# Batch 0's v cast by the DMA, its q and k on the other queue, and the first two gate and value tiles begun on half of their channels

## The chip, the cores and the metric

The kernel runs on one core of one Trainium2 chip. The metric is the device time of one execution in microseconds (us). A kernel is run several times beside runs of the kernel before on the same chip. "Span" is the part of an execution that the profile covers, some 1.8 us less than its time.

The core's engines are TensorE (PE, with its weight loads as PEld), VectorE (DVE), ScalarE (ACT), GpSimd (POOL) and SyncE (SP). Two kinds of DMA queue matter. Loads issued from SyncE go to a hardware queue (q1 in the trace) and arrive as they are. Loads issued from GpSimd go to a software queue (q0), which can also cast fp32 to fp16 on the way.

## The reference

```python
# q, k, v: (8 batches, 8 heads, 576 rows, 64), fp32
kv  = einsum('bhsd,bhse->bhde', k, v)              # one 64x64 state per batch and head
o   = einsum('bhsd,bhde->bhse', q, kv)
x   = o / sqrt(mean(o*o over the head) + 1e-6) * g_norm
x   = x.transpose(0, 2, 1, 3).reshape(4608, 512)   # 512 channels = 8 heads x 64
h   = gelu(x @ w_gate) * (x @ w_val)               # 512 -> 1536, twice
out = x + sigmoid(x @ w_res) * (h @ w_out)         # 1536 -> 512
```

## The kernel before

One batch is one "block" of 512 tokens (rows 0 to 511 of its 576). The remaining 64 rows of all batches are gathered into a ninth block. While TensorE does the feed-forward work of block b, the attention of batch b+1 is slipped in between ("plan"). Only batch 0 has nothing before it to hide behind, so it is done in two halves of four heads each, and those first 26 us are what most of the change is about.

The loads of batch 0. All three tensors come as fp32 on SyncE's queue in halves; the remaining 64 rows of k and v come on GpSimd's queue, cast, as `kl` and `vl`:

```python
for half in range(2):
    lo, hi = half * HH, (half + 1) * HH
    for which, t in (("q", q), ("k", k), ("v", v)):
        nc.sync.dma_start(out=raw[0, which][:, lo:hi, :], in_=rows4(t, 0, lo, hi))
# ... g_norm, three small loads on SyncE
load_last_kv(0)          # kl, vl: k and v of rows 512 to 575, all eight heads, on GpSimd
```

k-times-v of a half needs five matmuls for each pair of heads: four over the 512 rows, then one over the remaining rows, in the same accumulation.

```python
for j in range(NJ):
    nc.tensor.matmul(ps, lhsT=k16[:, j, cs], rhs=v16[:, 2*pr : 2*pr+2, j*D : (j+1)*D],
                     start=(j == 0), stop=False)
nc.tensor.matmul(ps, lhsT=kl[:, cs], rhs=vl[:, cs], start=False, stop=True)
```

The order of the start, cut. `keep_warm(n)` issues n multiplications of zeros, which are to keep TensorE's clock up (a run below shows it, with a clock of 1.00 against 0.50):

```python
f_cast("q", 0, nc.scalar.copy)
f_cast("k", 0, nc.vector.tensor_copy)
f_qT(0)                                  # transposes of q
...
f_cast("v", 0, nc.gpsimd.tensor_copy)
keep_warm(3)
f_kv(0); f_kv_out(0)                     # k-times-v of half 0, masked
f_o(0, 0, 2, ...); f_o(0, 2, 2, ...)     # outputs of half 0
f_sq; f_red; f_sqrt; f_t                 # squares, sums, root, t = o / rms
f_cast("k", 1, nc.gpsimd.tensor_copy)
for i in range(len(WCS)):
    load_wgv(i)                          # weights of gate and value, on GpSimd
...
f_cast("v", 1, nc.vector.tensor_copy)
f_kv(1); f_kv_out(1)                     # half 1, its normalisation token block by token block
```

The first two gate and value tiles are then made for each token block j over all four channel chunks at once, after the block's transposes:

```python
for j in range(NJ):
    after(j)                             # transposes and evacuation of token block j
    for f in range(2):
        m_mm(tiles[2*f],     wg_c, f, blk, j, j + 1)    # 128x128, channels 0 to 511
        m_mm(tiles[2*f + 1], wv_c, f, blk, j, j + 1)
```

## Time and profile before

| | before |
|---|---|
| median, all runs beside the changed kernel | 375.12 us (374.72 to 375.77, 4 runs) |
| span of the profiled run, mean granted TensorE clock | 373.6 us, 0.993 |
| TensorE busy | 358.0 us, 96% |
| mask of half 0's k-times-v starts | 10.52 us |
| gate and value tile 2 starts (TensorE dense from here) | 26.55 us |
| block 1 starts | 64.78 us |

The last three rows are read from the time order of the instructions (start, length, instruction, and in brackets the idle time before it and what ended it); two of them are:

```profile
10.52 0.42 DVE L458 TENSOR_TENSOR kv<-kvp,mask 128x256 f16<-128x256 f32 x1 [3.42 <-PE kvp L168]
64.78 1.04 PE L286 MATMUL gps<-xT,wg 128*128 128x512 f16 x4
```

They cut the run into pieces that can be judged alone. Up to the mask it is loading that counts; from mask to tile 2 the chain of half 0, half 1 and normalisation; from tile 2 to block 1 the stalls around batch 1's attention. From the start of block 1 on, the kernel takes 308.8 us (373.6 - 64.78).

### The profile page before, as it was taken

How to read it: one execution, taken by the hardware profiler on the slowest of the kernel's cores; microseconds unless marked ns; L12 is line 12 of the kernel's file. 1: busy time of each engine (PE TensorE's matmuls, PEld its weight loads, DVE VectorE, ACT ScalarE, POOL GpSimd, SP SyncE). 2: the span in 40 equal slices, each digit the busy share in tenths (PEclk: the TensorE clock that was granted, in tenths of full speed). 3: DMA queues.
4: the chain of work that ended last, by engine and by line, in shares of the span. 5: the costliest groups of instructions: out<-in, count | busy, mean ns of one | idle time of the engine just before them, and what ended most of it. 6: DMA issues, size and time to landing. Idle time of an engine off the chain costs nothing.

```text
span 373.6 us, 5442 instructions
## 1 busy us (share of the span) xinstructions
PE 358.0 (96%) x2120; PEld 180.6 (48%) x2120; DVE 215.6 (58%) x427; ACT 153.2 (41%) x257; POOL 47.0 (13%) x65
## 2 busy tenths in 40 slices
PE   6779999999999999999999999999999999999993
PEld 2554464554455455545464445444644444444441
DVE  2566448778546946584657664756478453343422
ACT  3563373453346344544364335533563333123310
POOL 3843140500050002200130005000000000000000
PEclk9899999999999999999999999999999999999998
DMA  9999997590159012901192029601000200020013
GB/s 246 187 202 197 198 200 74 81 221 2 58 107 141 0 56 63 182 5 56 61 172 18 28 84 133 58 31 56 30 0 2 84 29 2 28 80 7 0 43 70
DMA packets 49452, 30.76 MB, mean 82 GB/s; under 512 B 14098, under 2 KB 44818, under 8 KB 49426
## 3 DMA queue, kind: packets, MB, share of 16 engines
q0 software_dynamic: 40848, 17.83, 38.2%
q1 hardware_dynamic: 8578, 12.59, 9.6%
q8 instruction: 16, 0.26, 0.3%
q14 instruction: 10, 0.08, 0.1%
HBM read 38.80 MB, written 9.44 MB: 129 GB/s over the span
## 4 chain that ended last, share of the span: by engine, by line
PE 90%; DVE 5%; DMA 2%; ACT 1%; issue 1%; SPq 0%; DVEq 0%
PE gps L286 25%; PE vps L286 24%; PE fps L331 24%; PE rps L318 8%; DMA qf<-in_q_dram 2%; PE xtp L260 2%; PE kvp L161 2%; PE qtp L151 2%; PE op L190 2%; DVE t L501 1%; DVE pf L337 1%; DVE ss L485 1%; ACT xT L521 1%; PE orp L208 0%; PE kvp L168 0%
## 5 line engine op out<-in xcount | busy, mean ns | idle before, releaser
L286 PE MATMUL gps<-xT,wg 128*128 128x512 f16 (+1 forms) x456 | 112.6, 368 | 2.0 <-ACT xT L521 1.5
L275 DVE TENSOR_TENSOR hid<-ge,vps 128x512 f16<-128x512 f16 x108 | 73.6, 685 | 68.0 <-PE vps L286 67.8
L286 PE MATMUL vps<-xT,wv 128*128 128x512 f16 (+1 forms) x456 | 111.9, 368 | 0.0
L274 ACT ACTIVATE ge<-gps 128x512 f16<-128x512 f32 x108 | 64.5, 598 | 99.7 <-PE gps L286 92.9
L331 PE MATMUL fps<-wo,hid 128*128 128x512 f16 x432 | 99.6, 379 | 0.0
L286 PEld LDWEIGHTS <-wv 128*128 128x128 f16 x456 | 43.6, 98 | 50.2 <-issue 0.2
L331 PEld LDWEIGHTS <-hid 128*128 128x128 f16 x432 | 42.0, 98 | 49.3
L286 PEld LDWEIGHTS <-wg 128*128 128x128 f16 x456 | 41.8, 98 | 42.7 <-issue 2.6
L337 DVE SCALAR_TENSOR_TENSOR pf<-th,fps 128x512 f32<-128x512 f32 x36 | 24.5, 688 | 59.4 <-PE fps L331 59.4
L318 PE MATMUL rps<-wr,xT 128*128 128x512 f16 x144 | 36.9, 379 | 0.1
L327 ACT ACTIVATE th<-rps 128x512 f32<-128x512 f32 x36 | 21.5, 598 | 37.7 <-PE rps L318 37.7
L261 ACT ACTIVATE xT<-xtp,gcol 128x512 f16<-128x512 f16 x32 | 20.5, 685 | 37.6 <-PE xtp L260 37.6
L99 POOL DMA_DIRECT2D qraw<-in_q_dram x7 | 6.3, 894 | 162.0 <-DVE q L106 126.8
L342 DVE SCALAR_TENSOR_TENSOR osb<-pf,t 128x512 f32<-128x512 f32 x36 | 24.9, 691 | 1.1
L184 DVE TENSOR_REDUCE ss<-sq 128x8 f32<-128x512 f32 x32 | 21.9, 686 | 5.5 <-ACT sq L183 3.0
L183 ACT ACTIVATE sq<-op 128x512 f32<-128x512 f32 x28 | 16.8, 598 | 12.0 <-PE op L190 12.0
L318 PEld LDWEIGHTS <-xT 128*128 128x128 f16 x144 | 13.2, 98 | 13.9 <-issue 1.5
L248 DVE TENSOR_TENSOR t<-op,ny 128x512 f16<-128x512 f32 x28 | 17.9, 683 | 0.3
L152 ACT COPY qT<-qtp 128x1024 f16<-128x1024 f16 x14 | 14.2, 1013 | 9.1 <-PE qtp L151 9.1
L161 PE MATMUL kvp<-v,k 128*128 128x128 f16 x128 | 10.9, 222 | 3.3 <-POOL v L434 2.2
L267 DVE TENSOR_TENSOR t<-t,g 128x512 f16<-128x512 f16 x36 | 13.5, 418 | 0.0
L190 PEld LDWEIGHTS <-qT 128*128 128x128 f16 x112 | 8.6, 98 | 6.6
(82 smaller groups left out, 203.4 us busy)
## 6 DMA issues: line engine op xcount, KB each, us to landing
out_dram<-osb SPq DMA_DIRECT2D x32, 256.0 KB, 2.3
qraw<-in_q_dram POOLq DMA_DIRECT2D x7, 512.0 KB, 6.0
kraw<-in_k_dram POOLq DMA_DIRECT2D x7, 512.0 KB, 7.9
v<-in_v_dram POOLq DMA_DIRECT2D x7, 512.0 KB, 9.8
wo<-in_moe_w_out_dram POOLq DMA_DIRECT2D x3, 512.0 KB, 13.8
qf<-in_q_dram SPq DMA_DIRECT2D x2, 512.0 KB, 7.6
kf<-in_k_dram SPq DMA_DIRECT2D x2, 512.0 KB, 6.5
vf<-in_v_dram SPq DMA_DIRECT2D x2, 512.0 KB, 7.8
```

The lines of the kernel that those rows point to most:

```text
L161: nc.tensor.matmul(ps, lhsT=k16[:, j, cs], rhs=v16[:, 2 * pr : 2 * pr + 2, j * D : (j + 1) * D], start=(j == 0), stop=False,)
L184: nc.vector.tensor_reduce(out=st[b]["ss"][:, j, :], in_=sq, op=ALU.add, axis=mybir.AxisListType.X)
L248: nc.vector.tensor_tensor(out=t_t[blk][:, jj, :].rearrange("p (h d) -> p h d", h=H), in0=s["o"][j].rearrange("p (h d) -> p h d", h=H), in1 ...
L261: nc.scalar.activation(out=xT_t[blk][:, :, jj * P : (jj + 1) * P], in_=ps, func=AF.Copy, scale=gcol)
L274: nc.scalar.activation(out=ge, in_=gps, func=AF.Gelu)
L275: nc.vector.tensor_tensor(out=hids[blk][:, f, :], in0=ge, in1=vps, op=ALU.mult)
L286: nc.tensor.matmul(ps[:, j0 * P : j1 * P], lhsT=w[:, cc, :], rhs=xT_t[blk][:, cc, j0 * P : j1 * P], start=(cc == 0), stop=(cc == NP - 1),)
L318: nc.tensor.matmul(rps, lhsT=xT_t[blk][:, cc, j * P : (j + 1) * P], rhs=wr16[:, cc, :], start=(cc == 0), stop=(cc == NP - 1),)
L327: nc.scalar.activation(out=th, in_=rps, func=AF.Tanh, scale=0.5)
L331: nc.tensor.matmul(fps, lhsT=hids[blk][:, f, j * P : (j + 1) * P], rhs=wo16[:, f, :], start=(f == 0), stop=(f == NF - 1))
L337: nc.vector.scalar_tensor_tensor(out=pf, in0=th, scalar=1.0, in1=fps, op0=ALU.add, op1=ALU.mult)
L342: nc.vector.scalar_tensor_tensor(out=osb, in0=pf, scalar=0.5, in1=t_t[blk][:, j, :], op0=ALU.mult, op1=ALU.add)
```

## The change

The intent has three parts. (1) *Loads*: v is cast by the DMA on GpSimd's queue, which takes two casts off GpSimd and VectorE; q and k stay on SyncE's queue. (2) *Start*: the accumulation of tiles 0 and 1 over channels 0 to 255 (half 0) is put under the normalisation of half 1, so that only channels 256 to 511 remain for the four serial rounds. (3) *Plan*: batch 1's attention becomes one clump after the residual matmuls of block 0.

```diff
-        for which, t in (("q", q), ("k", k), ("v", v)):
+        for which, t in (("q", q), ("k", k)):
             nc.sync.dma_start(...)
+    load_v0(0)                        # v, heads 0 to 3, on GpSimd, cast by the DMA
     ... g_norm, on SyncE
-    load_last_kv(0)
     make_identity(nc, ident32)
+    load_last_kv(0)
+    load_v0(HH)                       # v, heads 4 to 7
 ...
-    f_cast("v", 0, nc.gpsimd.tensor_copy)
-    keep_warm(3)
+    keep_warm(6)
     f_kv(0)
     f_kv_out(0)
 ...                                  (k's second half: cast by VectorE, q's by GpSimd)
-    f_cast("v", 1, nc.vector.tensor_copy)
+    keep_warm(5)
     f_kv(1)
 ...                                  (half 1 is normalised in two pairs, not four blocks)
+        for f in range(2):
+            m_mm(tiles[2 * f], wg_c, f, 0, 0, NJ, 0, 2)       # 128x512, channels 0 to 255
+            m_mm(tiles[2 * f + 1], wv_c, f, 0, 0, NJ, 0, 2)
+        for j in range(NJ):
+            f_xT(1, j, 1, pattn, "at")
+            f_xT_out(1, j, 1, j == NJ - 1)
+            for f in range(2):
+                m_mm(tiles[2 * f], wg_c, f, 0, j, j + 1, 2, NP)
+                m_mm(tiles[2 * f + 1], wv_c, f, 0, j, j + 1, 2, NP)
 ...
+    def attn_plan_1():                (both transposes of q, k-times-v and the remaining
+        ...                            rows in one slot; the multiplications by g in block 1)
```

More of the change, by code (lines that the diff above doesn't have):

```diff
@@ L281, in w_of, with m_mm @@
         return ws[i][:, :, o : o + P]
-    def m_mm(ps, ws, f, blk, j0, j1):
+    def m_mm(ps, ws, f, blk, j0, j1, c0=0, c1=NP):
         w = w_of(ws, f)
-        for cc in range(NP):
+        for cc in range(c0, c1):
             nc.tensor.matmul(
@@ L290, in m_mm @@
                 start=(cc == 0),
-                stop=(cc == NP - 1),
+                stop=(cc == NP - 1 and j1 == NJ),
             )
@@ L301, in m_gval @@
         m_act(blk, f, gps, vps)
-    def m_gval_first(blk, after):
-        hids[blk] = hidp.tile([P, NF, NJ * P], FP16, tag="hid", name="hid")
-        tiles = [pmoe.tile([P, NJ * P], FP32, tag="mm", name=n) for n in ("gps", "vps", "gps", "vps")]
-        for j in range(NJ):
-            after(j)
-            for f in range(2):
-                m_mm(tiles[2 * f], wg_c, f, blk, j, j + 1)
-                m_mm(tiles[2 * f + 1], wv_c, f, blk, j, j + 1)
-        for f in range(2):
-            m_act(blk, f, tiles[2 * f], tiles[2 * f + 1])
     def m_res(blk, j):
@@ L378, with load_v0 @@
     raw[0, "q"] = stage.tile([P, H, NJ * D], FP32, name="qf")
-    for which in "kv":
-        t = hidp.tile([P, NF, NJ * P], FP16, tag="hid", name=which + "f")
-        t = t.rearrange("p a b -> p (a b)").bitcast(FP32)[:, 0 : H * NJ * D]
-        raw[0, which] = t.rearrange("p (h x) -> p h x", h=H)
-    for half in range(2):
-        lo, hi = half * HH, (half + 1) * HH
-        for which, t in (("q", q), ("k", k), ("v", v)):
-            nc.sync.dma_start(out=raw[0, which][:, lo:hi, :], in_=rows4(t, 0, lo, hi))
+    t = hidp.tile([P, NF, NJ * P], FP16, tag="hid", name="kf")
+    t = t.rearrange("p a b -> p (a b)").bitcast(FP32)[:, 0 : H * NJ * D]
+    raw[0, "k"] = t.rearrange("p (h x) -> p h x", h=H)
+    for lo in (0, HH):
+        for which, t in (("q", q), ("k", k)):
+            nc.sync.dma_start(out=raw[0, which][:, lo : lo + HH, :], in_=rows4(t, 0, lo, lo + HH))
+    def load_v0(lo):
+        nc.gpsimd.dma_start(out=b16_t[0, "v"][:, lo : lo + HH, :], in_=rows4(v, 0, lo, lo + HH))
+    load_v0(0)
     gcol = consts.tile([P, 1], FP32, name="gcol")
@@ L428, with f_cast @@
     first = {}
-    def f_cast(which, half, copy):
-        hs = slice(half * HH, (half + 1) * HH)
-        dst, src = b16_t[0, which], raw[0, which]
-        if which == "v":
-            copy(out=dst[:, hs, :], in_=src[:, hs, :])
-        else:
-            copy(
-                out=dst.rearrange("p j h d -> p h j d")[:, hs, :, :],
-                in_=src.rearrange("p h (j d) -> p h j d", j=NJ)[:, hs, :, :],
-            )
+    def f_cast(which, lo, hi, copy):
+        hs = slice(lo, hi)
+        copy(
+            out=b16_t[0, which].rearrange("p j h d -> p h j d")[:, hs, :, :],
+            in_=raw[0, which].rearrange("p h (j d) -> p h j d", j=NJ)[:, hs, :, :],
+        )
     def f_qT(half):
@@ L494, in f_sqrt, with f_rinv @@
         nc.scalar.activation(out=rms0[at], in_=s0["ss"][at], func=AF.Sqrt, bias=eps_col, scale=1.0 / D)
+    def f_rinv(half, j0, n):
+        hs = slice(half * HH, (half + 1) * HH)
+        nc.vector.reciprocal(out=rinv0[:, j0 : j0 + n, hs], in_=rms0[:, j0 : j0 + n, hs])
     def f_t(half, j0, n):
@@ L498, in f_t @@
         ps = first["o", half, j0]
-        nc.vector.reciprocal(out=rinv0[:, j0 : j0 + n, hs], in_=rms0[:, j0 : j0 + n, hs])
         for j in range(n):
@@ L506, in f_t, with f_xT_tile, f_xT_pe @@
             )
-    def f_xT(half, j0, n, pool, tag):
-        first["xT", half, j0] = ps = pool.tile([P, 2, n, P], FP16, tag=tag, name="xtp")
+    def f_xT_tile(half, j0, n, pool, tag):
+        first["xT", half, j0] = pool.tile([P, 2, n, P], FP16, tag=tag, name="xtp")
+    def f_xT_pe(half, j0, n):
+        ps = first["xT", half, j0]
         for j in range(n):
@@ L513, in f_xT @@
                 nc.tensor.transpose(ps[:, e2, j, :], t0[:, j0 + j, cc * P : (cc + 1) * P], ident)
+    def f_xT(half, j0, n, pool, tag):
+        f_xT_tile(half, j0, n, pool, tag)
+        f_xT_pe(half, j0, n)
     def f_xT_out(half, j0, n, on_vector):
@@ L523 @@
     keep_warm(10)
-    f_cast("q", 0, nc.scalar.copy)
-    f_cast("k", 0, nc.vector.tensor_copy)
+    f_cast("q", 0, HH, nc.scalar.copy)
     f_qT(0)
+    f_cast("k", 0, HH, nc.vector.tensor_copy)
     f_qT_out(0, nc.scalar.copy)
     f_qT_out(1, nc.vector.tensor_copy)
-    f_cast("v", 0, nc.gpsimd.tensor_copy)
-    keep_warm(3)
+    keep_warm(6)
     f_kv(0)
     f_kv_out(0)
-    f_cast("q", 1, nc.scalar.copy)
+    keep_warm(2)
     f_o(0, 0, 2, pmoe, "mm")
     f_o(0, 2, 2, pmoe, "mm")
+    f_cast("q", HH, H, nc.gpsimd.tensor_copy)
+    for i in range(len(WCS)):
+        load_wgv(i)
     f_sq(0, 0, 2)
+    f_sq(0, 2, 2)
     f_red(0, 0, 2)
+    f_red(0, 2, 2)
+    f_sqrt(0, 0, 2)
+    f_sqrt(0, 2, 2)
+    keep_warm(4)
     f_qT(1)
     f_qT_out(2, nc.scalar.copy)
-    f_qT_out(3, nc.vector.tensor_copy)
-    f_cast("k", 1, nc.gpsimd.tensor_copy)
-    for i in range(len(WCS)):
-        load_wgv(i)
-    load_qr(0)
-    f_sqrt(0, 0, 2)
-    f_t(0, 0, 2)
-    f_sq(0, 2, 2)
-    f_red(0, 2, 2)
-    f_sqrt(0, 2, 2)
-    keep_warm(8)
-    f_cast("v", 1, nc.vector.tensor_copy)
+    f_qT_out(3, nc.scalar.copy)
+    f_cast("k", HH, H, nc.vector.tensor_copy)
+    f_rinv(0, 0, 2)
+    f_t(0, 0, 2)
+    keep_warm(5)
     f_kv(1)
@@ L555 @@
     f_xT_out(0, 0, 2, False)
+    f_rinv(0, 2, 2)
     f_t(0, 2, 2)
-    for j in range(NJ):
-        f_o(1, j, 1, pattn, "at")
-    f_sq(1, 0, 1)
-    f_sq(1, 1, 1)
-    f_red(1, 0, 1)
-    f_sqrt(1, 0, 1)
-    f_t(1, 0, 1)
-    keep_warm(2)
-    f_xT(0, 2, 2, pmoe, "mm")
-    f_sq(1, 2, 1)
-    f_xT(1, 0, 1, pattn, "at")
-    f_xT_out(1, 0, 1, False)
-    f_red(1, 1, 1)
-    f_sqrt(1, 1, 1)
-    f_t(1, 1, 1)
-    f_xT_out(0, 2, 2, False)
-    f_sq(1, 3, 1)
-    f_red(1, 2, 1)
-    def first_chunk(j):
-        if j == 1:
-            f_xT(1, 1, 1, pattn, "at")
-            f_xT_out(1, 1, 1, False)
-            f_sqrt(1, 2, 1)
-            f_t(1, 2, 1)
-            f_red(1, 3, 1)
-        elif j == 2:
-            f_xT(1, 2, 1, pattn, "at")
-            f_sqrt(1, 3, 1)
-            f_xT_out(1, 2, 1, False)
-            f_t(1, 3, 1)
-            nc.scalar.preload_act_table_set("gelu_and_others")
-        elif j == 3:
-            f_xT(1, 3, 1, pattn, "at")
-            f_xT_out(1, 3, 1, True)
-            nc.vector.memset(ones16, 1.0)
-            nc.vector.tensor_copy(out=grow16, in_=grow[:, None, :].to_broadcast([1, H, D]))
-            for t in last_kv[1]:
-                nc.vector.memset(t[R:P], 0.0)
-            for t in qtr:
-                nc.vector.memset(t, 0.0)
@@ new lines, with first_gval @@
+    f_o(1, 0, 2, pattn, "at")
+    f_o(1, 2, 2, pattn, "at")
+    f_sq(1, 0, 2)
+    f_sq(1, 2, 2)
+    f_xT(0, 2, 2, pattn, "at")
+    f_xT_out(0, 2, 2, False)
+    f_red(1, 0, 2)
+    f_sqrt(1, 0, 2)
+    f_red(1, 2, 2)
+    f_sqrt(1, 2, 2)
+    f_rinv(1, 0, 2)
+    f_t(1, 0, 2)
+    f_rinv(1, 2, 2)
+    f_t(1, 2, 2)
+    keep_warm(6)
+    def first_gval():
+        hids[0] = hidp.tile([P, NF, NJ * P], FP16, tag="hid", name="hid")
+        tiles = [pmoe.tile([P, NJ * P], FP32, tag="mm", name=n) for n in ("gps", "vps", "gps", "vps")]
+        for f in range(2):
[4 more added lines that the diff above has]
+            f_xT_out(1, j, 1, j == NJ - 1)
+            if j == NJ - 1:
+                nc.scalar.preload_act_table_set("gelu_and_others")
+            for f in range(2):
+                m_mm(tiles[2 * f], wg_c, f, 0, j, j + 1, 2, NP)
+                m_mm(tiles[2 * f + 1], wv_c, f, 0, j, j + 1, 2, NP)
+        for f in range(2):
+            m_act(0, f, tiles[2 * f], tiles[2 * f + 1])
+        load_qr(0)
+        nc.vector.memset(ones16, 1.0)
+        nc.vector.tensor_copy(out=grow16, in_=grow[:, None, :].to_broadcast([1, H, D]))
+        for t in last_kv[1]:
+            nc.vector.memset(t[R:P], 0.0)
+        for t in qtr:
+            nc.vector.memset(t, 0.0)
@@ L605, in g_rows, with attn_plan_1 @@
         nc.vector.tensor_copy(out=g16, in_=ps)
+    def attn_plan_1():
+        b = 1
+        o = [lambda j=j: a_o(b, j) for j in range(NJ)]
+        t = [lambda j=j: a_t(b, j) for j in range(NJ + 1)]
+        x = [lambda j=j: a_xT(b, j) for j in range(NJ + 1)]
+        plan = {
+            NF - 1: [lambda: by_token(b, "q")],
+            NF: [lambda: by_token(b, "k")],
+            NF + 3: [
+                lambda: attn_begin(b),
+                lambda: a_qT(b, 0),
+                lambda: a_qT(b, 1),
+                lambda: load_batch(b + 1),
+                lambda: a_kv(b, 0, NP),
+                lambda: a_rem_qT(b),
+            ],
+            NF + 4: [lambda: a_rem_o(b), o[0]],
+            NF + 5: [o[1]],
+            NF + 6: [o[2]],
+            NF + 7: [o[3]],
+            NF + 8: [lambda: a_norm(b), t[0], t[1], t[2], t[3], t[4]],
+            2 * NF + 1: [x[0], x[1]],
+            2 * NF + 2: [x[2], x[3]],
+            2 * NF + 3: [x[4]],
+        }
+        return plan, [lambda j=j: a_x(b, j) for j in range(NJ + 1)]
     def attn_plan(b):
@@ L636 @@
         if blk == 0:
-            slots = [lambda: m_gval_first(0, first_chunk), None]
+            slots = [first_gval, None]
             slots += [lambda f=f: m_gval(0, f) for f in range(2, NF)]
@@ L645 @@
             slots += [lambda j=j: m_out(blk, j) for j in range(NJ)]
-            for j, f in enumerate(late):
-                plan[j] = [f]
+            for j, fs in enumerate(late):
+                plan[j] = list(fs)
             late = []
-        if blk + 1 < B:
+        if blk == 0:
+            new_block(1)
+            more, rows = attn_plan_1()
+            for i, fs in more.items():
+                plan.setdefault(i, []).extend(fs)
+        elif blk + 1 < B:
             new_block(blk + 1)
             for i, fs in enumerate(attn_plan(blk + 1)):
-                plan.setdefault((NF - 1 if blk == 0 else 0) + i, []).extend(fs)
+                plan.setdefault(i, []).extend(fs)
         for s in range(len(slots)):
@@ L658 @@
             if blk == 0 and s == 2:
+                nc.gpsimd.dma_start(out=wr16, in_=moe_w_res.rearrange("(cc p) c -> p cc c", p=P))
                 load_batch(1)
-                nc.gpsimd.dma_start(out=wr16, in_=moe_w_res.rearrange("(cc p) c -> p cc c", p=P))
                 for f in range(0, NF, 4):
@@ L664 @@
         if blk == 0:
-            late = stores
+            late = [[g] for g in stores] + [[] for _ in range(NJ)]
+            for j, g in enumerate(rows):
+                late[j + 2].append(g)
 _INS = ['q', 'k', 'v', 'g_norm', 'moe_w_gate', 'moe_w_val', 'moe_w_out', 'moe_w_res']
```

## The prediction

> **What bounds the kernel now.** I first read the busy shares of the page.
>
> ```profile
> PE 358.0 (96%) x2120; PEld 180.6 (48%) x2120; DVE 215.6 (58%) x427; ACT 153.2 (41%) x257; POOL 47.0 (13%) x65
> ```
>
> TensorE has work in 358.0 of 373.6 us. The dense feed-forward work in the middle is not shortened by this change, so what can be won is TensorE's idle time and the start, where part of its "work" is filler (multiplications of zeros that keep its clock up). The table of stretches shows where the idle time lies (columns: stretch, length, busy us and instructions of PE, PEld, DVE, ACT, POOL, granted clock, DMA share, GB/s written).
>
> ```profile
> 0.00:9.50 9.50, 6.00 (x22) 2.38 (x23) 2.61 (x10) 2.91 (x3) 3.23 (x9) 1.00 0.93 248
> 9.50:19.50 10.00, 7.01 (x63) 4.99 (x63) 6.24 (x16) 5.03 (x11) 8.22 (x11) 0.83 1.00 184
> 19.50:26.55 7.05, 5.14 (x73) 4.25 (x73) 3.98 (x14) 4.76 (x11) 3.02 (x4) 1.00 1.25 203
> 26.55:44.40 17.85, 17.85 (x81) 7.72 (x80) 9.75 (x19) 6.41 (x11) 4.36 (x6) 1.00 1.45 197
> 44.40:60.00 15.60, 14.68 (x116) 8.34 (x116) 9.34 (x24) 8.05 (x15) 4.70 (x6) 1.00 1.41 193
> 60.00:80.00 20.00, 19.43 (x136) 10.43 (x137) 15.63 (x28) 10.50 (x16) 4.69 (x6) 1.00 0.61 105
> ```
>
> Until 26.55 us TensorE idles 3.50 + 2.99 + 1.91 = 8.4 us; then it is dense; between 44.4 and 80 it loses 0.92 + 0.57 = 1.5 us. The other idle time is the tail after 360 us, which the change does not touch. So two numbers matter: when the dense part (tile 2 of gate and value) begins, now 26.55, and the small stalls around the second batch's attention. The time order of the start says what makes it late (start, length, instruction, and in brackets the idle time before it and what ended it).
>
> ```profile
> 8.39 1.04 POOL L434 CAST v<-vf 128x1024 f16<-128x1024 f32 x1 [5.08 <-DMA vf<-in_v_dram]
> 9.48 0.38 PE L161 MATMUL kvp<-v,k 128*128 128x128 f16 x4 [2.19 <-POOL v L434]
> 12.26 0.79 POOL L121 DMA_DIRECT2D wg<-in_moe_w_gate_dram  x1
> 15.95 0.38 PE L161 MATMUL kvp<-v,k 128*128 128x128 f16 x4 [1.15 <-DVE v L434]
> 20.33 0.27 PE L286 MATMUL gps<-xT,wg 128*128 128x128 f16 x2 [0.45 <-ACT xT L521]
> 24.10 0.27 PE L286 MATMUL gps<-xT,wg 128*128 128x128 f16 x2 [0.62 <-ACT xT L521]
> 26.55 1.02 PE L286 MATMUL gps<-xT,wg 128*128 128x512 f16 x4
> ```
>
> The chain is: v lands and is cast, k-times-v, output of half 0, its normalisation; the cast of v's second half, k-times-v of half 1, and the same again; then four rounds of transpose, evacuation and 16 small matmuls. The weight loads leave POOL only at 12.26, behind the cast of k.
>
> **What the Trainium skill says.** "DMA: Bandwidth & Descriptors", section "Queues, rings and completion order": every DMA engine takes turns, packet by packet, between the queues that have work. So v on the other queue adds no bandwidth, but q and k no longer stand before it. No wait of the trace before isolates this. The same page, "Anatomy of one DMA — SWDGE (gpsimd) path", gives 2.0 us plus bytes / 436e3: 3.2 us for the 0.52 MB read by the first weight load; the trace's shortest is 3.7 us, in fair agreement. "TensorE: Matmul & The Clock Gate", Part 1, says idling halves the clock: the trace agrees, the granted clock is 0.50 in 10 to 13 us after 2.19 us of idling. It names a window of 3.4 us; here 2.2 us of complete idling was enough. "SBUF — State Buffer", "Who interferes with whom", says a two-port VectorE copy shuts GpSimd out, descriptors included; no row of this trace shows that, so I use it only for a rival.
>
> **The change, part by part.**
>
> *Loading.* Removed: v's casts (1.04 us on POOL, 1.00 on DVE). Batch 0 still reads 3 x 1.05 MB. Before, halves landed, as their casts or issue-to-landing times show, at about 4.65 (q), 5.95 (k), 8.38 (v), 9.9 (q), 11.25 (k), 12.7 us (v): 1.3 to 1.4 us per 0.52 MB, with about 1.2 us lost to the two small loads of the remaining rows, which landed at 9.3. After, with equal turns of two queues, I work out (estimate from those 1.4 us): q 4.9, v 6.5, k 7.5, remaining rows 8.9 to 9.3, q 10.2, v 11.7, k 12.4 us. k-times-v of half 0 then waits not for v but for the remaining rows, and ends near 9.3 to 9.7 at full clock (filler rises from 3 to 6) rather than 10.5: about 1 us earlier.
>
> *Half 0 to half 1.* Mask 0.42, outputs 0.6, two squares of 0.6, two reductions of 0.69: VectorE is free at 12.4 to 12.7. Then k's second cast (0.69, now on VectorE), 1/rms and two t (0.20 + 0.75): 14.0 to 14.3. k-times-v of half 1 has run meanwhile, where before it began at 15.95; its mask ends near 14.5. That is 2.4 us earlier than 16.70 + 0.42 = 17.12, of which 1.0 is the cast of v.
>
> *Normalising half 1.* Before, four tile chains; now two pairs: square, reduction, root, 1/rms, two t. On ScalarE the evacuation of half 0's second transposes must follow the squares and ends at 16.9; TensorE then does channels 0 to 255 of tiles 0 and 1, 8 matmuls of 128x512 at 0.216 = 1.7 us, until 18.65, under the normalisation (t of token block 0 near 17.8, of the last near 19.1). So transposes find t ready. The weights they need are issued after q's cast, at about 11.3 instead of 12.26, and by the 3.7 to 4.9 us of before land at 15 to 17.0: just in time.
>
> *The last rounds.* Four rounds remain in series on TensorE: transpose to evacuation 0.31, evacuation 0.47, hand-over 0.05, now 8 small matmuls instead of 16, 0.47 instead of 0.93: 1.30 each. 18.65 + 3 x 1.30 + 1.18 (the last evacuates on VectorE in 0.35) = 23.7. Tile 2 needs a PSUM buffer, freed by the first gelu (0.55 after its sum is complete, now only in the last round): 24.1. Gain: 26.55 - 24.1 = **2.4 us**. TensorE's arithmetic is unchanged (64 x 0.055 = 3.5 us against 1.7 + 1.8).
>
> *Batch 1's attention.* It now starts at the fourth slot after tile 11, in one clump, with five feed-forward steps (5.2 us) between last output and first transpose; before, these were the waits:
>
> ```profile
> 45.85 0.62 PE L151 MATMUL qtp<-ident,q 128*128 128x128 f16 x8 [0.30 <-DVE q L106]
> 59.52 0.40 PE L260 MATMUL xtp<-ident,t 128*128 128x128 f16 x4 [0.43 <-DVE t L248]
> 60.12 0.40 PE L260 MATMUL xtp<-ident,t 128*128 128x128 f16 x4 [0.20 <-DVE t L248]
> ```
>
> These 0.93 us, and 0.1 us at 44.4 where the residual weight had just landed (it is now loaded before batch 1), should go: 1.0 us. The first t took 4.65 us from the last output, inside 5.2. Against it, the clump has four ScalarE copies (2 x 1.01 + 0.75) after a tanh of 0.6, 3.4 us, beside about 3.1 us of TensorE work before the remaining rows' outputs: a new wait of 0.3. Net **0.7 us**. The multiplications by g move into block 1: five of 0.42 us on a 58% busy VectorE, hidden.
>
> Sum: 2.4 + 0.7 = 3.1 us; 374.98 - 3.1 = 371.9.
>
> **Rivals.** (a) *The weights become the bound.* The DMA runs from 14 to 58 us without a pause. If tile 2 begins earlier and weights do not, TensorE waits. For: the first pair is just in time above. Against: the third pair landed near 25 and 27 and was used at 30.4 and 31.3; 4 us of slack exceed the 2.4. If it happens, most of the gain is lost: 374. (b) *v's cast load is slow or blocked*, sharing turns with q and k, so k or the remaining rows land 1 to 2 us later than estimated and k-times-v starts no earlier: 373 to 374. For: the remaining rows stand behind v in one queue; short packets. Against: TensorE has filler and the second half is limited by VectorE. (c) *The first part costs less than I allow*: rounds overlap and loads land earlier, tile 2 at 22.5: 370. (d) *The clumped attention turns into stalls of over 1 us* in 45 to 50 us, as ScalarE and VectorE serve it in series: 373. For: 16 transposes and 20 matmuls with no feed-forward matmul between. Against: PSUM has the buffers.
>
> **Range and chances.** The start can be off by 1.5 us either way, attention by 0.7, mostly together with the loads: 369.5 to 374.3. Over 2% faster would need 367.5, a gain of 7.5 of the 9.9 us idle outside the tail, by a change that leaves the four serial rounds: 0.03. Slower than 382 would need a wait of 10 us: 0.01. Within 2%: 0.96.
>
> **What would show it.** Right: k-times-v of half 0 ends by 9.7, no half clock around 10 to 13 us; first weights issued near 11.3; first 128x512 gate matmul near 17, tile 2 near 24.1, rounds of 1.3 us; no wait on the transposes of batch 1; tile 11 not waiting for a weight load. Wrong: TensorE waiting on DMA of weights or v; remaining rows landing after 10; waits of over 0.5 us after the residual matmuls.

## The result, and the profile after

The changed kernel took 376.02 us in the median (375.08 to 376.27, 4 runs) against 375.12. The ratio is 1.0018, with a 95% interval of 0.9995 to 1.0041: the same within 2%, and not the 3.1 us faster that were predicted. Ratios in this document are the mean time of one kernel's runs over that of the other's of the same rounds, so they are not quite the ratio of the quoted medians.

The busy shares of the kernel after:

```profile
PE 359.3 (96%) x2106; PEld 180.5 (48%) x2106; DVE 214.1 (57%) x422; ACT 152.4 (41%) x253; POOL 47.3 (13%) x66
```

VectorE has a little less to do (215.6 to 214.1 us): v's second cast is gone, but k's second cast has come to it from GpSimd. TensorE is 1.3 us busier, with ten more filler matmuls (33 instead of 23). Neither says anything of the time. The table of stretches of the kernel after does, with the columns of the one in the prediction (stretch, length, busy us and instructions of PE, PEld, DVE, ACT, POOL, granted clock, DMA share, GB/s):

```profile
0.00:9.50 9.50, 6.56 (x28) 2.60 (x28) 2.52 (x10) 2.91 (x3) 4.02 (x11) 1.00 0.92 225
9.50:19.50 10.00, 7.29 (x60) 4.88 (x61) 4.65 (x12) 3.98 (x9) 9.03 (x12) 0.83 1.40 190
19.50:26.55 7.05, 5.35 (x48) 3.21 (x45) 3.06 (x8) 3.69 (x8) 2.43 (x3) 1.00 1.24 206
26.55:44.40 17.85, 17.07 (x84) 7.80 (x84) 10.58 (x23) 6.98 (x12) 3.60 (x5) 1.00 1.45 197
44.40:60.00 15.60, 15.60 (x121) 8.95 (x120) 8.27 (x21) 8.73 (x15) 4.69 (x6) 1.00 1.31 169
```

Two things are to be seen. TensorE is busy in all of 44.40 to 60.00, where it lost 0.92 us before. And the stretch from 26.55, which was dense before, now has 0.78 us of idle time: the start runs over into it. TensorE is busier than before up to 26.55 and yet later, because part of that is filler and part ran at half clock.

The time order of the kernel after shows where (start, length, instruction, and in brackets the idle time before it and what ended it):

```profile
8.52 0.38 PE L161 MATMUL kvp<-v,k 128*128 128x128 f16 x4 [0.86 <-DMA v<-in_v_dram]
10.17 0.76 POOL L121 DMA_DIRECT2D wg<-in_moe_w_gate_dram  x1
11.87 0.22 PE L168 MATMUL kvp<-vl,kl 128*128 128x128 f16 x1 [2.97 <-DMA vl<-in_v_dram]
12.66 0.42 DVE L446 TENSOR_TENSOR kv<-kvp,mask 128x256 f16<-128x256 f32 x1 [5.69 <-PE kvp L168]
20.69 0.59 PE L286 MATMUL gps<-xT,wg 128*128 128x512 f16 x2
23.25 0.27 PE L286 MATMUL gps<-xT,wg 128*128 128x128 f16 x2 [0.56 <-ACT xT L519]
24.54 0.27 PE L286 MATMUL gps<-xT,wg 128*128 128x128 f16 x2 [0.56 <-ACT xT L519]
27.93 1.02 PE L286 MATMUL gps<-xT,wg 128*128 128x512 f16 x4 [0.35 <-ACT ge L274]
```

v is there at 8.5 us, about an us sooner than v's cast ended before. But the fifth matmul of the first pair of heads, the one over the remaining rows, waits 2.97 us for `vl`, a load of 64 rows. The mask therefore starts at 12.66 where before it started at 10.52, and what follows is late: the first 128x512 gate matmul comes at 20.69, tile 2 at 27.93, which is 1.38 us later than before. The weights are issued at 10.17, sooner than forecast, and two rounds lie 24.54 - 23.25 = 1.29 us apart, as forecast.

The chain of what ended last (start, length, what) begins with that load, and not with one of q as before:

```profile
3.35 8.47 DMA vl<-in_v_dram
```

It was issued at 3.35 us and took 8.47 us to land. In the three us after it TensorE's clock is halved:

```profile
12.00:15.00 3.00, 3.00 (x19) 1.90 (x18) 0.86 (x2) 1.06 (x2) 3.00 (x5) 0.50 1.48 187
```

In the second piece the change gained. These are the transposes of q, those of t, and the start of block 1 in the kernel after; none carries a bracket, so the waits of before are gone (counted from start to start, 0.10 us within the transposes of t and 0.21 before block 1 are left):

```profile
49.08 1.06 PE L151 MATMUL qtp<-ident,q 128*128 128x128 f16 x16
61.37 0.72 PE L260 MATMUL xtp<-ident,t 128*128 128x128 f16 x8
64.53 1.02 PE L286 MATMUL gps<-xT,wg 128*128 128x512 f16 x4
```

From tile 2 to block 1 it is 64.53 - 27.93 = 36.60 us, against 64.78 - 26.55 = 38.23 before: 1.63 us saved. From the start of block 1 on, both kernels take the same 308.8 us (373.6 - 64.78 and 373.3 - 64.53). So in the profiled runs the change loses 1.38 us at the start and gains 1.63 in the attention, and 0.25 are left; the spans are 373.3 and 373.6. The other three runs of the kernel after had spans of 374.1 to 374.5, about an us more than its profiled run, so the timed difference is +0.9 us in the median. Its interval contains no difference at all, and I do not explain it further.

### The profile page after: what moved, and what is told of

It is laid out like the page before. It is cut to its first block, busy times and chain, and to the rows that moved or that the text cites. A ratio compares the mean times of both kernels' runs of the same rounds, so it can differ in the third digit from the quotient of the medians.

```text
span 373.3 us, 5398 instructions
## 1 busy us (share of the span) xinstructions
PE 359.3 (96%) x2106; PEld 180.5 (48%) x2106; DVE 214.1 (57%) x422; ACT 152.4 (41%) x253; POOL 47.3 (13%) x66
## 4 chain that ended last, share of the span: by engine, by line
PE 93%; DMA 2%; DVE 1%; issue 1%; ACT 1%; POOL 0%; DVEq 0%; POOLq 0%
PE gps L286 25%; PE fps L319 25%; PE vps L286 24%; PE rps L306 9%; DMA vl<-in_v_dram 2%; PE xtp L260 2%; PE kvp L161 2%; PE qtp L151 2%; PE op L190 2%; PE idle L411 1%; DVE osb L330 1%; PE kvp L168 1%; PE orp L208 1%; PE op L459 0%; ACT xT L519 0%
## 5 line engine op out<-in xcount | busy, mean ns | idle before, releaser
L411 PE MATMUL idle<-zeros 128*128 128x512 f16 x33 | 11.1, 487 | 1.2 <-DVE zeros L389 1.2
```

## The experiments

Why did 64 rows take 8.5 us? The trace's packets give the first hint: in 7 to 9.5 us both queues are at work. The lines give a queue, its packets, the MB written and the time its packets took, as a share of 16 engines. First the kernel before, then the one after:

```profile
q1 hardware_dynamic: 722, 0.71, 94.4%
q0 software_dynamic: 434, 0.05, 32.8%
```

```profile
q1 hardware_dynamic: 586, 0.58, 84.1%
q0 software_dynamic: 574, 0.10, 48.4%
```

After, the queues moved 586 and 574 packets: turn by turn, but 0.58 MB against 0.10. A packet of q or k writes 1 KB, one of the remaining rows 128 bytes (64 fp16 values of one head), and both cost a turn. `kl` and `vl` are 64 rows times 8 heads, so 512 packets each; half of v is 512 too. Before, only the 1,024 small packets were in the software queue. Now 512 packets of v stand before them. What is more, the software queue moved no packet before about 4.9 us in any of the kernels, though its first load is issued at 1.24 us: in 2 to 5 us of these two only the hardware queue appears, with 937 packets before and 938 after.

**Theory**: the start is late because the remaining rows stand behind v in a queue that starts late and gets only every second turn, as long as q and k are on the other one. **Rivals**: the order within the queue alone is to blame; the clock after the wait; VectorE holding GpSimd's descriptors back; or the new chain after the mask is slow itself.

All times in the following are medians; "mask" and "tile 2" are start times in the profiled run.

### The rows ahead of v

```diff
+    load_last_kv(0)
     load_v0(0)
 ...
-    load_last_kv(0)
     load_v0(HH)
```

> Edit: the two small loads of the remaining rows of k and v go ahead of v's first half in the POOL queue. Theory (shares of two queues): the POOL queue still has to move the same three loads while q and k take every other turn, so the last of the three lands where it did (11.9 us), only it is now v; k-times-v of half 0 ends near 12.6, tile 2 begins at 27.5 to 28.3, time within 0.3% of the changed kernel. Rival (mere order, the small loads should have gone first): the rows land near 9.3 and v near 10, tile 2 near 26, about 2 us less than the changed kernel.

376.02 us, ratio 1.0008 (0.9988 to 1.0027). Now v is the last to land:

```profile
11.81 0.58 PE L161 MATMUL kvp<-v,k 128*128 128x128 f16 x4 [3.57 <-DMA v<-in_v_dram]
```

Mask at 13.07, tile 2 at 29.05, an us later than in the changed kernel. Tile 2 was expected at 27.5 to 28.3, so it came later than forecast, but the last of the three loads landed at 11.77, as the theory had it (11.83 in the changed kernel). The order within the queue is not the cause by itself: half 0 needs 1,536 packets from it either way.

### The second halves of q and k behind the rows, in the same queue

```diff
-    (q and k, heads 4 to 7, on SyncE)
+    (the same two loads on GpSimd, between load_last_kv(0) and load_v0(HH))
```

> Edit: the second halves of q and k leave the SP queue and are issued on POOL behind the remaining rows, so nothing but q and k of half 0 shares turns with v and the rows. Theory (the second halves take the turns that the remaining rows need): v lands at 6.5 to 7.5, the last rows at 9 to 9.8 instead of 11.87, k-times-v of half 0 ends at 9.7 to 10.4 instead of 12.6, tile 2 begins at 25.3 to 26.3 instead of 27.93, about 2 us (0.5%) less than the changed kernel. Rival (a casting load is slow by itself): v stays at 8.5, the rows at 11 or later, no gain.

374.58 us, ratio 0.9974 (0.9956 to 0.9991); mask 12.27, tile 2 27.63. The software queue had no company any more, and yet k-times-v started only at 9.90 and the matmul over the rows at 11.57. The expectation was missed. Moving the loads also changed their packets (4 KB instead of 1 KB), so this run cannot say which of the two it measured. I count it as inconclusive; a later run does it without this side effect.

### The old loads of v with all the rest of the change

```diff
+    (v, fp32, in two halves on SyncE after q and k, as before; the rows alone on GpSimd)
+    f_cast_v(0, HH, nc.gpsimd.tensor_copy)
     keep_warm(6)
     f_kv(0)
 ...
+    f_cast_v(HH, H, nc.vector.tensor_copy)
     keep_warm(5)
     f_kv(1)
```

> Edit: batch 0's loads and the casts of v as in the kernel before (fp32 on SP, v cast on POOL and VectorE, rows first on POOL), all else as in the changed kernel. Theory: rows land at 9.3 and v is cast by 9.45; k-times-v of half 0 ends at 10.0 to 10.5; the cast of v's second half costs 1.0 us on VectorE; tile 2 at 26.2 to 26.8, about 1.3 us less than the changed kernel. Rival (the new order of the two halves itself costs the time): tile 2 stays at 27.5 or later.

373.93 us, ratio 0.9959 (0.9941 to 0.9977). The first line is k-times-v of half 0, the second tile 2:

```profile
9.45 0.38 PE L161 MATMUL kvp<-v,k 128*128 128x128 f16 x4 [1.66 <-POOL v L426]
...
26.22 1.02 PE L286 MATMUL gps<-xT,wg 128*128 128x512 f16 x4 [0.35 <-ACT ge L274]
```

With v's load and casts as they were, the start is again 1.7 us earlier than in the changed kernel (26.22 against 27.93). So the loss comes from moving v, and this version, with a cast that the change had removed, is the faster one.

The run also shows how little the new start gives by itself. From half 0's mask to tile 2 it is 26.22 - 10.20 = 16.02 us here and 26.55 - 10.52 = 16.03 in the kernel before. And from half 1's mask to tile 2 it is 27.93 - 17.89 = 10.04 us in the changed kernel (10.04 here too), but 26.55 - 16.70 = 9.85 before: beginning the first tiles on half of their channels did not shorten this stretch. It did so only in the last version below, with overlapped rounds (23.25 - 14.71 = 8.54).

### Half 0 without the remaining rows (a wrong result, on purpose)

```diff
-                stop=False,
+                stop=(j == NJ - 1 and b == 0 and pr < 2),
             )
+        if b == 0 and pr < 2:
+            return
         nc.tensor.matmul(ps, lhsT=kl[:, cs], rhs=vl[:, cs], start=False, stop=True)
```

> Edit: k-times-v of half 0 of batch 0 leaves out the 64 remaining rows (wrong result on purpose), so that it waits for v alone; loads unchanged. Theory (this one wait of 2.97 us is the step that failed): it ends at 9.1 instead of 12.6 and all that follows moves, until the second halves of k (11.3) and v (13.0) hold it: tile 2 at 24.2 to 25.2, 2.8 to 3.7 us less than the changed kernel. Rival (half clock and filler set the pace, or another load is just behind): tile 2 at 26.5 or later.

372.05 us, ratio 0.9897 (0.9876 to 0.9918). The result is off by a relative 0.091, as it must be: two pairs of heads lack 64 rows. Only two tiny matmuls are gone, and with them the wait for the rows:

```profile
9.38 0.61 PE L161 MATMUL kvp<-v,k 128*128 128x128 f16 x8 [1.74 <-DMA v<-in_v_dram]
...
24.93 1.02 PE L288 MATMUL gps<-xT,wg 128*128 128x512 f16 x4 [0.35 <-ACT ge L276]
```

The clock stays at 1.00 in 12 to 15 us, the mask comes at 10.02, tile 2 at 24.93: three us earlier than in the changed kernel. With this single wait removed the kernel lands near the time that was predicted for the change (371.9), though tile 2 is 0.8 us later than its predicted 24.1. From mask to tile 2 it is 14.91 us, less than the 16.03 of before, so the new chain after the mask is not what is slow.

### The new plan alone, on the kernel before

```diff
+    def attn_plan_1():  ...          (and wr16 loaded before batch 1, as in the change)
-                plan.setdefault((NF - 1 if blk == 0 else 0) + i, []).extend(fs)
+                plan.setdefault(i, []).extend(fs)
```

> Edit: the kernel before with only the new placing of batch 1's attention (clump after the residual matmuls, five steps before its transposes, residual weight loaded before batch 1, g rows moved into block 1). From the traces: tile 2 begins at 26.5 as before, and the way from tile 2 to block 1 shrinks from 38.23 to about 36.6 us, so 1.6 us less than the kernel before (373.5). Rival (it is worth the 0.7 us of my prediction, or only pays behind the new start): 374.3 or more.

374.10 us in 6 runs, ratio 0.9947 (0.9933 to 0.9960). Tile 2 starts at 26.66, as before, and block 1 here:

```profile
63.25 1.02 PE L286 MATMUL gps<-xT,wg 128*128 128x512 f16 x4
```

That is 63.25 - 26.66 = 36.59 us, 1.64 less than before and the same as in the changed kernel. By the ratio it is 0.0053 of 375.8 = 2.0 us. This part of the change is good, alone or together, and worth over twice what I had given it.

### Filler against the halved clock

```diff
-    keep_warm(6)
+    keep_warm(26)
     f_kv(0)
```

> Edit: the changed kernel with 26 instead of 6 filler matmuls ahead of k-times-v of half 0, so that TensorE is busy from 6.2 to about 11.8 us and its clock does not fall during the wait for the rows. Rival theory under test (the halved clock, seen as 0.50 from 12 to 15 us, and not the wait itself costs the time): tile 2 at 26.5 or earlier, 1.4 us or more gained. Main theory (the wait costs it): the clock stays at 1.00, the small matmuls after the wait shorten, but tile 2 moves by only 0.5 to 0.8 us, 27.1 to 27.4.

374.58 us, ratio 0.9966 (0.9951 to 0.9981). The clock is full after the wait:

```profile
12.00:15.00 3.00, 2.10 (x24) 1.38 (x23) 0.42 (x1) 0.46 (x1) 3.00 (x5) 1.00 1.08 132
```

The mask came 0.98 us later than in the changed kernel (13.64 against 12.66), as the rows themselves landed later in this trace (13.07 against 11.83 us), and tile 2 only 0.06 later (27.99 against 27.93). From mask to tile 2 it is 14.35 us instead of 15.27, so the halved clock had cost about 0.9 us. Neither forecast was met: tile 2 did not come sooner, and yet by the medians the run is 1.4 us faster than the changed kernel, the figure that stood for the rival. The profiles hide this, as the profiled run is the slowest of its four (375.11) and that of the changed kernel the fastest of its own (375.08). The mean granted clock of the four runs is 0.997 to 0.999, against 0.988 to 0.991 in the changed kernel, so the clock matters for the time, by more than the one profiled start shows. The halved clock followed the wait, though, and the wait itself stays; the kernel is still far from the prediction.

### Rows of half 0 only, ahead of v

```diff
+    load_last_kv(0, 0, HH)           # heads 0 to 3: 2 x 256 packets
     load_v0(0)
 ...
-    load_last_kv(0)
+    load_last_kv(0, HH, H)
     load_v0(HH)
```

> Edit: in the changed kernel the remaining rows are loaded by half of the heads: those of half 0 first on POOL (512 packets instead of 1024), then v's first half, then the other rows, v's second half. Theory (the software queue starts at 5.3 us and then moves one packet per turn, so what counts is the packets queued ahead of what half 0 needs: 1536 now, 1024 here): rows of half 0 by 7, v at 9 to 9.7, k-times-v of half 0 ends at 9.6 to 10.4 instead of 12.6, tile 2 at 24.8 to 25.6, 2.3 to 3.1 us less than the changed kernel, about 373. Rival (bytes, or the casting of v itself): v not before 11, tile 2 at 27 or later.

375.27 us (373.38 to 377.57, 6 runs), ratio 0.9979 (0.9948 to 1.001). The runs range from the highest time at a mean clock of 0.984 to the lowest at 1.000, so the median says little. The forecast of v's landing missed. Half 0 needs only 1,024 packets of the software queue now instead of 1,536, and yet k-times-v started only at 11.71, as with all rows ahead of it:

```profile
11.71 0.59 PE L164 MATMUL kvp<-v,k 128*128 128x128 f16 x4 [3.60 <-DMA v<-in_v_dram]
```

In that trace v (landed at 11.67) still shares the engines with the second halves of q and k (the last landed at 11.48). Fewer packets ahead did not help here. Why is not shown: in 8 to 9 us the software queue moved 162 packets, against 248 in the changed kernel and 175 of the other queue, so a count of packets alone does not foretell the landing.

### Does VectorE hold the software queue back?

Two runs asked it. In one, the fills that VectorE does during the first loads are moved behind the transposes of q; in the other, k's first cast goes from VectorE to ScalarE:

```diff
-    (fills of kl, vl, mask and eps at the start)
+    (the same fills after f_qT_out(1))
```

> Edit: the changed kernel with the fills of kl, vl, mask and eps on VectorE moved from 1.2 to 2.5 us to after 7 us. Question: in all runs the first packet of the software queue moves at 5.2 to 5.4 us, 4.1 us after its issue, where later loads take 1.7 us. If VectorE's fills block the writing of descriptors, it moves near 3 to 4 us here and v lands by 7.5; if it is a fixed start, it stays at 5.2 to 5.4 and v at 8.4.

```diff
-    f_cast("k", 0, HH, nc.vector.tensor_copy)
-    f_qT_out(0, nc.scalar.copy)
+    f_cast("k", 0, HH, nc.scalar.copy)
+    f_qT_out(0, nc.vector.tensor_copy)
```

> Edit: the changed kernel with k's first cast on ScalarE instead of VectorE (5.9 to 6.6 us), half 0's qT copies both on VectorE. Question: the second load of the software queue moves its first packets only at 7.0 us or later in every run. If VectorE's fp32 cast shuts GpSimd out while it should write descriptors, they start near 6 here, the last rows land 0.7 to 1 us earlier (10.9 to 11.2) and tile 2 begins near 27. If not, rows land at 11.6 to 12.1 as before.

Without the fills the software queue's first packet moved at 5.10 us, the matmul over the rows started at 12.07 (11.87 in the changed kernel), and the single run, of unknown state, took 375.4 us. With k's cast on ScalarE that matmul started at 12.18, and the time was 375.44 us (374.98 to 377.98), ratio 1.0005 (0.9975 to 1.0035). Neither brought the rows forward, so neither of these VectorE operations is what delays them.

### The second halves on their own queue, only later

```diff
     load_qk0(0)                       # q, k of heads 0 to 3, on SyncE
 ...
     f_qT_out(1, nc.vector.tensor_copy)
+    for which in "qk":                # one column filled: the loads must wait for it
+        nc.vector.memset(raw[0, which][:, HH : HH + 1, 0:1], 0.0)
+    load_qk0(HH)                      # heads 4 to 7, on SyncE, issued at 7.25 us
```

> Edit: the changed kernel with the second halves of q and k still on SP but issued only near 7.1 us (behind two one-column fills by VectorE after its qT copy), so that from 6 to about 8.5 us v and the remaining rows have the DMA engines to themselves and no other load is added to the POOL queue. If sharing turns with the second halves is what makes the rows late: v at 7.5 to 8, last rows by 9.3 to 9.9 instead of 11.87, tile 2 at 25.5 to 26.3, about 374. If the software queue is slow by itself in this phase, as the earlier run with the second halves behind it on POOL suggests (rows 11.57): rows at 10.8 or later and no gain.

This leaves queue, packets and order as in the change and only keeps the other queue empty while the rows are moved. The packets in 7 to 9.5 us show it (compare 574 and 586 above):

```profile
q0 software_dynamic: 1465, 0.34, 147.7%
q1 hardware_dynamic: 77, 0.00, 1.7%
```

The wait for the rows and tile 2:

```profile
9.51 0.22 PE L168 MATMUL kvp<-vl,kl 128*128 128x128 f16 x1 [0.75 <-DMA vl<-in_v_dram]
...
25.84 1.02 PE L286 MATMUL gps<-xT,wg 128*128 128x512 f16 x4 [0.35 <-ACT ge L274]
```

The rows landed at 9.47 instead of 11.83, tile 2 started 2.1 us earlier, and the time was 373.85 us, ratio 0.9975 (0.9951 to 0.9998). The same loads do not land alike in every trace: in the five traces that have the changed kernel's loads, the rows landed at 11.83, 11.94, 12.13, 12.87 and 13.07. The 2.4 us gained here are more than that scatter. This shows the theory for the rows: between v's landing and theirs lie 1.14 us instead of 3.35, so the small packets were late because they shared turns with 1 KB packets that nobody needed yet. It does cleanly what the inconclusive run above was meant to do; why that run's own rows were late is not answered.

For v the theory does not hold. v landed at 8.33 against 8.48 in the changed kernel, and not at the 7.5 to 8 that I expected. In 6 to 7 us the software queue moved 188 packets here, with the other almost silent (61), and 189 in the changed kernel beside 153. That v was 2 us later than predicted is thus not the doing of the second halves.

What remains of the gap to the 24.93 of the run without rows is the other side of the trade, the second halves of q and k, which now land late: the transposes of q's second half wait 1.47 us at 13.46 for its cast.

### A version that beats both

Two steps. First, v as fp32 on SyncE's queue again, cast by VectorE, the remaining rows of heads 0 to 3 alone on the software queue, and those of heads 4 to 7 after q's second cast:

```diff
+    (v, fp32, on SyncE; both casts on VectorE, the second after that of k)
+    load_last_kv(0, 0, HH)
 ...
     f_cast("q", HH, H, nc.gpsimd.tensor_copy)
+    load_last_kv(0, HH, H)
```

> Edit: the changed kernel with v in fp32 on the SP queue as in the kernel before, both its casts on VectorE, rows of half 0 first and alone on POOL, rows of half 1 issued only after POOL's cast of q. Theory (packets): rows by 6.7, v lands at 7.2 to 7.8, its cast ends near 8.3, k-times-v of half 0 ends at 8.7 to 9.2, tile 2 at 23.4 to 24.4, time 370.3 to 371.5, faster than both kernels. Rival: the second halves (k cast, v cast, rows of half 1 near 12.5) or the weights hold it: tile 2 at 25 or later, 372.5.

372.98 us (372.2 to 374.9, 6 runs), ratio 0.9929 (0.9909 to 0.9950). The mask starts at 9.58. By time this missed (370.3 to 371.5 was expected). The profiled run was the slowest of the six; in it the clock fell to 0.55 in 22 to 29 us, so its tile 2 (25.39) says little:

```profile
22.00:29.00 7.00, 5.95 (x29) 3.23 (x27) 3.13 (x9) 3.44 (x5) 1.56 (x2) 0.55 1.24 206
```

TensorE was busy for 5.95 of those 7 us. In its four rounds, from 20.11 to 24.34, stand four waits of half an us, one in each round. So the second step is to issue each round's transposes one round ahead, to fill those waits:

```diff
+        f_xT(1, 0, 1, pattn, "at")
         for j in range(NJ):
-            f_xT(1, j, 1, pattn, "at")
+            if j + 1 < NJ:
+                f_xT(1, j + 1, 1, pattn, "at")
             f_xT_out(1, j, 1, j == NJ - 1)
```

> Edit: the version with v in fp32 and rows by half (which measured 372.98) with each round's transposes issued one round ahead, so that their evacuation runs beside the matmuls of the round before. The four serial rounds of 1.28 us should become about 0.6 us each after the first, TensorE is busier, so its clock should not fall at 22 us as it did in the profiled run of that version: tile 2 at 22.4 to 23.4, time 369.3 to 370.8. Rival: the weights (third pair lands near 25.5 and 27.3) then hold tile 4, or the clock falls all the same: 371.5 or more.

371.88 us (370.76 to 372.66, 5 runs), ratio 0.9897 (0.9879 to 0.9916): still "same" at 2%, but about 3.9 us faster than the kernel before (0.0103 x 375.64), with a correct result. Tile 2 came where expected (23.25), the time not: 369.3 to 370.8 was forecast, and only the profiled run reached it. The rounds have one wait left at their begin and tile 2 is 3.3 us earlier than before:

```profile
20.06 0.27 PE L289 MATMUL gps<-xT,wg 128*128 128x128 f16 x2 [0.45 <-ACT xT L521]
23.25 1.02 PE L289 MATMUL gps<-xT,wg 128*128 128x512 f16 x4 [0.85 <-ACT ge L277]
```

## Why the prediction was wrong

| step of the prediction | predicted | measured | run that tells |
|---|---|---|---|
| v of half 0 lands | 6.5 us | 8.5 us | changed kernel |
| remaining rows land | 8.9 to 9.3 us | 11.8 us | changed kernel |
| k-times-v of half 0 ends | by 9.7 us, full clock | about 12.6 us, then clock 0.50 | changed kernel |
| the same, without that wait | | mask 10.02, clock 1.00; tile 2 24.93 | half 0 without rows |
| first weights issued | 11.3 us | 10.17 us | changed kernel |
| first 128x512 gate matmul | near 17 us | 20.69 us | changed kernel |
| one round | 1.30 us | 1.29 us | changed kernel |
| tile 2 starts | 24.1 us | 27.93 us | changed kernel |
| gain in the attention | 0.7 us | 1.63 us | changed kernel; plan alone 1.64 |

**The step that failed is the landing times on GpSimd's queue, "v 6.5" and above all "remaining rows 8.9 to 9.3".** I let the software queue move from its issue on, took equal turns of two queues to mean equal bytes, and so gave the rows the time of before although 512 packets of v had been put ahead of them. v landed at 8.48, so 2.0 of the 2.5 to 2.9 us were lost before the turn of the rows came. The rows then took 3.35 us more, and 1.14 when the other queue was kept empty. The trace of before held what was needed to see otherwise. Its software queue moves no packet before about 5.0 us (5.0 to 5.1 in that trace), and its 434 packets in 7 to 9.5 us write only 0.05 MB. Counted in packets, the 1,024 of the rows now stand behind 512 of v, with every second turn. The rule of turns that I took from the Trainium skill ("DMA: Bandwidth & Descriptors", "Queues, rings and completion order") agrees with the trace as long as both queues have packets ready: 574 and 586 in the same 2.5 us. (The page's packet is typically 9 to 17 descriptors; whether the trace counts the same packets is not shown.) I applied it to bytes.

**What the error cost.** The rows are 2.5 to 2.9 us later than predicted. "Filler rises from 3 to 6" was to hold the clock, but six multiplications cannot bridge a wait of 2.97 us; the halved clock added about 0.9 us, as the filler run showed. Together 3.4 to 3.8 us, against the 3.83 us by which tile 2 is late. The run without the rows' wait gives 27.93 - 24.93 = 3.0 us for both; the other 0.8 us stay when the wait is gone. A gain of 2.4 us became a loss of 1.38.

**What held.** The rounds came as worked out, and the weights sooner. Rival (a), that the weights become the bound, did not occur: no matmul of these first tiles waits for a weight load. The run without the rows' wait starts tile 2 at 24.93, 0.8 us late, and takes 372.05 us, near the predicted 371.9. That it comes so near is in part luck: the attention's larger gain, 0.9 us more than predicted, makes up for the late tile 2. One sum of the prediction is off (17.12 - 14.5 is 2.6 us, not 2.4), but nothing was built on it.

**The attention's gain was sized too small**: 1.63 instead of 0.7 us. The new wait of 0.3 us that I set against it did not appear (no idle time in 44.4 to 60), and each wait removed was worth more than its bracket. Measured from one start to the next, less the 0.216 us (128x512) or 0.056 us (128x128) between two starts where nothing waits, the waits before were 0.28, 0.47, 0.59, 0.36 and 0.30 us, 2.00 in all. I had counted the first four as about 1.0 of idle time and the fifth not at all. Idle time counts from the modelled end of the last matmul, which a following one would have overlapped: four matmuls of 128x512 are shown as 1.03 us long, but where nothing waits the next one starts 0.86 us after the first. After, 0.38 us are left (0.07, 0.10 and 0.21), and 2.00 - 0.38 = 1.62 is the gain. This error made up for 0.9 of the 3.8 us of the first one: without it the kernel would have been slower in the profile as well.

**The rivals.** Rival (b) described what happened, the remaining rows behind v in one queue of short packets, but with 373 to 374 us it was sized too small, as it reckoned with rows 1 to 2 us late and no lost clock. Rivals (c) and (d) did not occur.

**What stays open.** Why the software queue's first packet moves only at 5.0 us (neither VectorE's fills nor its cast), and why it then moves only some 190 packets in 6 to 7 us with or without the second halves beside it, so that v is late either way; why v and the rows stayed slow in the run with all second halves on the software queue, and v in the run with the rows by half; and why the changed kernel's other runs were an us longer than its profiled one.

## What to carry to other kernels

Before a load is moved to another queue, list everything that the first consumer waits for, the smallest loads too, and look at both queues: a small load behind the moved one inherits its whole delay. Here a new order within the queue gained nothing (376.02 us with the rows first), while holding back what was not needed yet on the other queue brought the rows 2.4 us forward. Look at packets beside bytes: 64 rows of 128 bytes per head are as many packets as half a tensor. A count of packets alone is no forecast, as the run with the rows by half showed. And read a wait before TensorE twice, once for its length and once for the clock after it.

## What the Trainium skill lacked or had wrong

- "DMA: Bandwidth & Descriptors", "Queues, rings and completion order": the turns at packet granularity agree with the counts, if the trace's packets are the page's, but the page does not say what follows for a mixture of sizes. With 586 packets against 574 in 2.5 us one queue wrote 0.58 MB and the other 0.10.
- The same page, "Anatomy of one DMA — SWDGE (gpsimd) path": its formula of 2.0 us plus bytes / 436e3 would give the remaining rows of v (128 KB read) an estimate of about 2.3 us; they took 8.47 us, behind 1,024 other packets and with every second turn. It has nothing on the first load of a program either: issued at 1.24 us, its first packet moved at about 5.0 us in every kernel.
- "TensorE: Matmul & The Clock Gate", Part 1: it names a window of 3.4 us for the clock to fall. Here 2.97 us of waiting gave a clock of 0.50 in 12 to 15 us, and 2.19 us in the kernel before 0.50 in 10 to 13, while after 1.74 us in the run without rows it stayed at 1.00.
- "SBUF — State Buffer", "Who interferes with whom": VectorE holding back GpSimd's descriptors was not seen. Moving the fills, or taking a cast off VectorE, left the matmul over the rows at 12.07 and 12.18 us (11.87 with them).
- No page that I read says that an idle time of the profile understates what its removal is worth: four waits that I had counted as about 1.0 us of idle time were 1.70 us from start to start.
